# A gated mix of a long convolution and linear attention: the inverse transform of the last channel groups turned by VectorE

## The chip, the cores and the metric

The kernel runs on one core of one Trainium2 chip. The metric is the device time of one launch in microseconds (us), as the median of several runs. The core has five engines that run side by side and meet at semaphores: TensorE (PE: matmuls, and PEld: its weight loads), VectorE (DVE), ScalarE (ACT), GpSimd (POOL) and SyncE (SP), which here only issues DMA transfers. SBUF is the on-chip memory of 128 partitions, PSUM the memory that TensorE writes its results to, DRAM the memory off the core.

## The reference

For a sequence `x` of 2048 steps and 512 channels:

```
g   = sigmoid(sum(x * gate_w))                                   # one number for each step
K   = real(sum_n C * exp(dt*A*l) * dt*B)                         # one kernel of 2048 taps for each channel
a   = irfft(rfft(x, 4096) * rfft(K, 4096))[:2048] + x * Dskip    # causal convolution along the steps
b   = linear attention: softmax features of q and k (32 heads of 16), num / den, then @ wo
out = g * a + (1 - g) * b
```

Data are bf16, sums on the chip f32.

## The kernel before

The convolution is done as a Fourier transform of 4096 points in two stages, in matmuls with small tables. The 512 channels are cut into sixteen **units** of 32 channels (`U` = 0 to 15), four units to a **quarter** (`Q` = 0 to 3). Of each unit the kernel `K` is built first (`kgen`): VectorE multiplies out a table `A` (steps A1, A2, and A3, a sum over two halves of `A`, L1109) and a table `R` (Rh, Rl), both from exponentials `E` (ScalarE, then El on VectorE) and sines `cs` (ScalarE), and TensorE contracts them into `kps`. The string `FOURS` names the units whose A3 is left out, with twice as many matmuls in its place. `kps` is evicted to `KD`, transformed by TensorE (`psA`, evicted to `XA`; `psB`, evicted to `XK`), and VectorE multiplies `XK` with the spectrum of `x`, read back from DRAM as `XUX` (steps t128, t64, t32; L1231, L1234).

Then comes the inverse transform, `transform`. Its first half is one matmul step, `psz`, evicted to `Zr`. Its second half (`psy`, many matmuls with the table `TJ`, 64 rows by 32 columns each) needs two indices of `Zr` exchanged inside blocks of 32 partitions. There are two ways to it:

- the **far** path: `Zr` is written to a DRAM tensor `Zd` (step zw) and read back in the other order as `ZT` (step zr). Quarters 0 to 2 take it in groups of 128 channels; the last quarter for units 12 and 13 together (64 channels) and for unit 14 (32 channels).
- the **narrow** path, for unit 15: 128 matmuls of 64 columns (`pszn`, L1301) give the result in the needed order at once, two evictions give `Z` (Zn), and 128 matmuls of 16 columns follow (`psyn32`, L1358), with two gate products (L1373).

At the end of either, VectorE multiplies by the gate (`ou`, L1367, L1370, L1373) into `xT`, from which the result is stored (L1384).

Attention runs beside it: projections and exponentials of the keys (`pk`, `Ek`), the sums of the exponentials (`Zk`), values (`vp`, evicted to `vb`, then `vr`), and four blocks of queries, the last of which (`late`) is finished near the end (`opsL`, `bpsL`, evictions bs3 and bsg, stores L992). The string `ZPS` names the steps of the keys in which TensorE adds four columns to one first, so that VectorE's reduction (L735) has 512 elements; the others have two reductions of 1024 elements (L732). At the start the channels of `x` are turned (`xT`), copied (`UDp`, step udc), transformed (`psA`, evicted to `XAu`; `psB`, evicted to `xst`, step XU) and written to DRAM (`XUd`).

All steps are nodes of a `Plan`. The order in which they are issued is written out by hand in the string `ORDER`, two characters for a node; each engine works off its nodes in that order. Most evictions may go to ScalarE or VectorE, and `SIDES` has a digit for each: 0 is the first engine named, 1 the second. `RINGS` chooses between PSUM rings in the same way. Rings of buffers (`take` and `drop`) bound how far a step can run ahead; `ax` has one buffer, `Zr` two.

The stores of results name the queues `("SP", "ACT")`; in the code the choice `SP` goes to GpSimd's queue for all stores but the last.

Of the kernel before, what the change touches and what calls it, by code (L numbers as in the profile page):

```python
# [11 lines left out]
ALU = mybir.AluOpType  # L12
# [58 lines left out]
class Plan:  # L71

    DIGITS = "0123456789abcdefghijklmnopqrstuvwxyzABCDEFGHIJKLMNOPQRSTUVWXYZ-_"
    ORDER = ("0405060B0C0D0H0d0e0f0y0z0A190s0t0u0708090I0J0M000L11120g0h0i0j0k0l0K0102030_2R0S0T100W0U0Y2x0V130P0Q2S0N2T0X2y2U142V0O0R"
             "160Z0m0n0o0a0b0c0p0q0r152X2J2Z170-0v0w0x182-1a1b1y1c0E0F0G1n1d2W2K1o2_1e1w1z2Y1H1A2D1x301f2E2L1p1I1E1J1S312M2B2C1g1C3235"
             "361B37381P2F2G2H1q1r1s2I33341F2N2O2v2P2Q2z4C393b3c4J4L3a3d3f4Y4K4M1t1u1v1R3g4-4Z3e4_4N3h4Q3j504R3i4O3l513k4P4S4U3n4V4W1Y"
             "1N3o3m5357584T4X1D5b1G5254593R5c553S5d5e5i5m5j5n3p3r3s5f5g561O5a5q5r5s5h5t5o5x5y1L5k1T4D2w4E3q5u5v5B5l4F5p3w5C3y3x3z3t3u"
             "3v5F5H3D5w5D3F5z1Z5A5E3E5G5U5W5I1U5J5V3A3B3C3G3T5X5M5Q5K3K5R5L4G5S5N3M5_1V1M5Y5O5Z5-63645P5T1Q67606169653N2A683L62663U1W"
             "6a6m6n6o6p1h1i1j3V3W6b1K6c3X6q3Y3Z6r1k1l1m6d3_3-416e6s401X1-3H3I3J4243451_272021442829223O3P3Q47482a4649232d2e4b2b2f244a"
             "2c2o4c252g4g4i2h4h2i4j6f2p2j4d4e4f4k4l4m2q2k2l264n4p4o2m4q2s6t2r4u4v6g2n4r4s4t6i2t4w6h6u4x2u6j8m6k6x8q6v8k8o6y6l6z4y4z4A"  # L80
             "6w6A6B8l8p8n8r8s4B8w8x6G8t8y6I8u4H8C4I6J8v8D8z8A8Z8E6K6L8I6M6H6F6C6D6E8B6N8F8-8J7d6O8_7e6P9b9c9d8Q8R6Q7M8G7f7N6R7g7h6S9k"
             "9l9m6T8H8K7i7O7j8S8L8W937P8T7k8M8N8Xan7Q6U6V6W8Uao7l8V8O7m9e9f9g948P6X6Y6Z7R7n7o8Y907p7S6_7071aeaf91ag92a47q6-7r7s7tap95"
             "7Taha8a972a5ai96akaaat73a675ab77979878ajal999aaua7ac7u7v7w7x74am7976aqaras9n7U9o9vadav9p9waK7C7VaEaw9q7WaL7aaB7b9xaQaM7X"
             "7Y9raRaC7y7z7A7D9y9z9h9i9j7Z9D9Eb5b6b7c5c6aFbX9F7c7Eb_7B9L9Mc0axayaDaH7G9NbYc19A9B9C7IaG9GaI9HazaAaJ7F7H7J7-7_80b-818283"
             "84898bc38c8aaNbZaO9s9t9uaPaSc2aTc7858687c4888d9O8f8gc88ececfaYaZa-7K7Lcbc9cc9Pck8haU8ia_b0b18jcBaVca9I9J9KaWaXcdcgclchcC"
             "b8bgb99Q9R9Sba9T9U9VcsctcicHcjbhbobpdYcDbicId-dZeUcmd_bbbjcncybce0bweV9Ze1cvcwbxb2b3b4cVcWcXe2bkbdbebf9W9X9Ycxco9-cue3e4"
             "czblbmbnbqcpcqdOe5creLcAcEeMbycFa0e6e7e8a1dSa2dTa3brcGcJbsbzcK9_eWeNeOcLcPcQcRe9eaebbAeceRcMcNdPedeeefegcOc_dUbtbubvd0eh"
             "bBbCbDcScTcUePeSeid1eQd7d8dQdfe-dVeTbEbFbGd2d9daeXdge_cYcZc-bHbIbJd3d4d5d6dbdndRdcdddeeYbKdhdWdoezeAeBdieZeCeDeEdXbLdpdj"
             "dkdldmbMf0f1dqdrfAfBfDfEf2f4bNg1f5fCf3fGbOfFg2f6f7fefHdBf8bPfffgdsdtdufIfJg7g3eIeJeKbQf9dvdwdxfafKdydzdAfhfidCg4dEdFfLfb"
             "fcfdfMg8fjfkfldGeFeGeHdHfmfnfog5fNg6fOejekfPfpfqfreldDg9gadLdMdNfQgbgcepdIdJdKemgdgeeneogffRfSfTfUbUbVbWeqbRbSbTggfsfVfW"  # L90
             "fXgighgjftgkglgmgngoeresfYfZf-fxfyfzewexeyfufvfwgqf_gpgreteuevg0gvgwgxgsgtgu")
    SIDES = ("101110000101100010001000101110100001101100001011100000000000000000100010010100101001000010000000000000000000000000000000"
             "00000000000000000000000110110000000000000000011000001")
    RINGS = ("000111101111001111000000000000000000000000100000000000000010001110100000101010101101010110011001010100110010011001111001"
             "11110")
# [714 lines left out]
def plan_queries(P, nc, g, psum, r):  # L810
# [14 lines left out]
    def block(b, late, yn=()):  # L825
# [163 lines left out]
        if late:  # L989
            def st(h):  # L990
                for c in (2 * h, 2 * h + 1):
                    nc.gpsimd.dma_start(out=g.out2d[:, 0:384].rearrange("(q j c) d -> c q j d", q=32, j=16, c=4)[c][:, 4 * b:4 * b + 4],  # L992
                                      in_=xT[32 * c:32 * c + 32, 4 * b:4 * b + 4, 0:3, :].rearrange("p j a d -> p j (a d)"))
            for h in range(2):
                P.dma("outL", 1.2, 2.0, lambda h=h: st(h), on, move=0.8, cnt=2, eng=("SP", "ACT"))
# [61 lines left out]
def plan_conv(P, nc, g, psum, r):  # L1057
# [132 lines left out]
    def transform(XA, ready, Q, off, nd, far, Ls, last, co=0, free=True, split=False):  # L1190

        F = Bag()
        ng, ns, nj, nt = nd // 2, 1024 // nd, min(16, 1024 // nd) if far else 8, min(32, 2048 // nd)
        do = slice(off, off + nd)
        nh, w = max(1, nd // 64), min(nd, 64)
# [4 lines left out]
        if far:  # L1200
            byrow = nd > 64
            F.Zd = g.dram.tile([32, 4, 32, nd] if byrow else [4, 32, 32, nd], BF16, name=f"Zd{Q}_{off}")
        tn, zn, rn, wn = [], [], [], []
        for r0 in range(0, 32, ns):
# [24 lines left out]
            def tt(k=None, r0=r0, box=box, end=end):  # L1229
# [11 lines left out]
                if k != 0:  # L1241
                    box.XK = None
                    if end:
                        F.t = None
                    if not far:
                        F.tt = box.t.rearrange("p k (r d) -> p k r d", d=nd)
                        box.t = None
# [8 lines left out]
            if not far:  # L1256
                continue

            def fi(box=box):
                box.ps = psum([128, 2, 512], "psz")  # L1260
                for hb in range(2):
                    for k in range(2):
                        nc.tensor.matmul(box.ps[:, hb, :], lhsT=fc.TIp[:, k].rearrange("p h a t -> p (h a t)"), rhs=box.t[:, k, 512 * hb:512 * hb + 512],  # L1263
                                         start=(k == 0), stop=(k == 1))
                box.t = None

            def fe(box=box):
                box.Z = g.fpool.tile([128, ns, nd], BF16, name="Zr", tag="Zr", bufs=g.P.k["Zr"])
                o, i = box.Z[:].rearrange("p r d -> p (r d)"), box.ps[:].rearrange("p h z -> p (h z)")
                if nd == 128:  # L1270
                    o, i = box.Z[:].rearrange("p r (h c) -> p h r c", h=2), box.ps[:].rearrange("p h (r c) -> p h r c", c=64)
                box.ps = None
                return o, i

            def fw(r0=r0, box=box):
                if byrow:
                    nc.sync.dma_start(out=F.Zd[r0:r0 + ns].rearrange("r x t d -> (x t) r d"), in_=box.Z[:])
                else:
                    nc.sync.dma_start(out=F.Zd[:, :, r0:r0 + ns, :].rearrange("x t r d -> (x t) r d"), in_=box.Z[:])
                box.Z = None  # L1280
            z = P.add("PE", "psz", fi, [tn[-1]] + ([z] if r0 else []), take=[psq, "Zr"], drop=(["r8"] if (r0 + ns) % nt == 0 else []), rw=("TI", ""))
            zn.append(evict("Zr", fe, [z] + zn[-1:]))
            wn.append(P.dma("zw", 0.45, 2.0, fw, [zn[-1]], drop=["Zr"], move=0.9))
# [10 lines left out]
        def iz(k2, box=box):  # L1294
# [9 lines left out]
            if k2:  # L1304
                F.tt = None
# [325 lines left out]
```

## Time and profile before

| | us |
|---|---|
| median of 3 runs | 260.62 |
| lowest, highest | 259.82, 261.87 |
| the profiled execution | 260.65 |
| its span, first to last instruction | 258.9 |
| VectorE busy | 228.8 (88%) |
| ScalarE busy | 224.5 (87%) |
| TensorE busy | 195.5 (76%) |
| GpSimd busy | 20.0 (8%) |

The span is what the trace covers; the time of the execution is 1.75 us longer. "Busy" of an engine counts instructions that work, not waits or the issuing of transfers (POOL's transfers are counted here as its instructions). In the slices of the profile each digit is the busy share of a fortieth of the span, in tenths. In the timeline a row gives start, duration, engine, line, operation, what is written and read, and in brackets how long the engine sat idle before it and what ended the wait; "issue" means that it waited for nothing that the profile shows. In the groups, the columns behind the shapes are the count, the busy time in all, the mean in ns of one, and the idle time before them.

### The profile page before, as it was taken

The page shows a single profiled execution, that of the slowest core. Times are in us where ns is not written, and L with a number is a line of the kernel's source. Part 1 is how long each engine was busy: PE and PEld are TensorE (multiplying, and loading weights), DVE is VectorE, ACT ScalarE, POOL GpSimd, SP SyncE. Part 2 cuts the span into 40 slices and gives each one's busy share as a digit, 9 for nine tenths or more (in the row PEclk, how much of TensorE's full clock was granted, in tenths as well). Part 3 has the DMA queues.
Part 4 walks back from the last instruction along what each step waited for, and adds up shares of the span by engine and source line. Part 5 has one row for each costly group of instructions (what it writes and reads, how often), then busy time and mean ns, then how long its engine had stood idle before and what let it go on. Part 6 is the DMA issues. An engine that isn't in the chain of part 4 may idle for free. (4 is left out here: it accounts for less than half of the span.)

```text
span 258.9 us, 10101 instructions
## 1 busy us (share of the span) xinstructions
PE 195.5 (76%) x4512; PEld 133.2 (51%) x4512; DVE 228.8 (88%) x308; ACT 224.5 (87%) x312; POOL 20.0 (8%) x37
## 2 busy tenths in 40 slices
PE   0558899999963787689648748688988589979832
PEld 0558664665643533246437434464775456856621
DVE  6798889797899998999999999999989999978711
ACT  7989979998999999999999999999997999766210
POOL 5540000000000000000000000000000000000770
PEclk9999999999998589999997997999999999999975
DMA  6799300073710578304632348615578988896792
GB/s 195 132 189 203 77 4 1 5 228 81 227 39 0 165 206 246 122 4 120 171 98 69 90 135 231 179 36 166 129 153 231 239 186 225 214 251 130 172 197 44
DMA packets 62139, 36.19 MB, mean 140 GB/s; under 512 B 42768, under 2 KB 57296, under 8 KB 61712
## 3 DMA queue, kind: packets, MB, share of 16 engines
q1 hardware_dynamic: 60272, 33.58, 52.4%
q0 software_dynamic: 768, 1.84, 3.1%
q8 instruction: 35, 0.57, 1.0%
q10 hardware_dynamic: 1056, 0.13, 0.3%
q14 instruction: 8, 0.07, 0.1%
HBM read 22.17 MB, written 13.37 MB: 137 GB/s over the span
## 5 line engine op out<-in xcount | busy, mean ns | idle before, releaser
L1098 DVE TENSOR_TENSOR A<-Ctab,Dtab 128x2048 bf16<-128x2048 bf16 x32 | 38.6, 1220 | 1.2 <-PE kps L179 1.2
L68 ACT ACTIVATE cs<-args 128x1024 bf16<-128x1024 f32 x32 | 31.3, 1073 | 0.0
L1384 POOL DMA_DIRECT2D out_dram<-xT x12 | 7.7, 649 | 225.0 <-ACT xT L145 223.4
L179 PE MATMUL kps<-R,A 128*32 128x64 bf16 x1536 | 17.6, 202 | 6.2 <-DVE A L1109 1.4
L179 PEld LDWEIGHTS <-A 128*32 128x32 bf16 x1536 | 15.8, 117 | 10.2 <-DVE R L1120 2.9
L1120 DVE TENSOR_TENSOR R<-E,cs 128x2048 bf16<-128x2048 bf16 x16 | 19.4, 1218 | 0.0
L1116 DVE TENSOR_TENSOR R<-E,cs 128x2048 bf16<-128x2048 bf16 x16 | 19.3, 1220 | 0.1
L1263 PE MATMUL psz<-t,TI 128*128 128x512 bf16 x60 | 16.2, 396 | 3.0 <-ACT cs L68 1.6
L145 ACT CAST XK<-psB 128x1024 bf16<-128x1024 f32 (+1 forms) x17 | 16.8, 1016 | 0.9 <-PE psB L192 0.8
L145 ACT CAST Zr<-psz 128x1024 bf16<-128x1024 f32 x15 | 15.6, 1040 | 2.1 <-ACT cs L68 0.6
L1231 DVE TENSOR_TENSOR t<-XUX,XK 128x2048 bf16<-128x2048 bf16 x14 | 17.1, 1219 | 0.0
L68 ACT ACTIVATE E<-args 128x1024 bf16<-128x1024 f32 x16 | 17.0, 1065 | 0.0
L68 ACT ACTIVATE Eq<-pq 128x512 bf16<-128x512 f32 (+1 forms) x28 | 16.8, 696 | 0.2 <-PE pq L839 0.2
L68 ACT ACTIVATE Ek<-pk 128x512 bf16<-128x512 f32 x32 | 16.7, 602 | 0.2
L753 PE MATMUL vp<-WW,xT 128*128 128x512 bf16 x64 | 16.8, 395 | 0.0
L612 PE MATMUL psB<-XAu,TB 64*128 64x128 bf16 x256 | 11.3, 250 | 6.2 <-ACT XAu L145 4.1
L839 PE MATMUL pq<-xT,Wqp 128*128 128x512 bf16 x64 | 15.4, 380 | 0.3 <-ACT E L68 0.3
L145 ACT CAST XA<-psA 128x1024 bf16<-128x1024 f32 x15 | 15.2, 1053 | 0.4 <-PE psA L186 0.4
L705 PE MATMUL pk<-WW,xT 128*128 128x512 bf16 x64 | 15.2, 380 | 0.0
L612 PEld LDWEIGHTS <-TB 64*128 64x128 bf16 x256 | 9.7, 111 | 9.5 <-issue 9.0
L762 DVE TENSOR_TENSOR vr<-vb,vr 128x1024 bf16<-128x1024 bf16 x16 | 10.6, 688 | 3.0 <-ACT vr L68 2.7
L186 PE MATMUL psA<-W,KD 128*64 128x128 bf16 x256 | 10.0, 223 | 4.3 <-ACT XK L145 1.7
(208 smaller groups left out, 511.2 us busy)
## 6 DMA issues: line engine op xcount, KB each, us to landing
XUX<-XUd SPq DMA_DIRECT2D x32, 256.0 KB, 4.4
XUd<-xst SPq DMA_DIRECT2D x8, 512.0 KB, 3.3
ax<-apd SPq DMA_DIRECT2D x16, 256.0 KB, 4.9
Zd<-Zr SPq DMA_DIRECT2D x15, 256.0 KB, 4.5
ZT<-Zd SPq DMA_DIRECT2D x12, 256.0 KB, 4.7
UD<-in_A_u_dram SPq DMA_DIRECT2D x16, 128.0 KB, 4.7
XUd<-xst SPq DMA_DIRECT2D x8, 256.0 KB, 3.9
wqk<-in_B_wqkv_dram SPq DMA_DIRECT2D x1, 1024.0 KB, 6.7
```

What stands on the lines that cost most here:

```text
L68: return self.nc.scalar.activation(**kw)
L145: self.nc.scalar.copy(out=o, in_=i)
L179: nc.tensor.matmul(kps[32 * dj:32 * dj + 32, g4, e, :], lhsT=A[:, d // 4, 32 * ka:32 * ka + 32, d % 4], rhs=R[:, kr, d, :], start=(i == 0) ...
L612: nc.tensor.matmul(box.ps[:, c2, sl, :], lhsT=fc.TB[rows, b0:b0 + 2].rearrange("p a b -> p (a b)"), rhs=X.t[rows, k, r0 + sl].rearrange("p ...
L705: nc.tensor.matmul(box.ps[:], lhsT=xT[:, st, kt, :], rhs=g.WW[:, kt, :], start=(kt == 0), stop=(kt == 3))
L753: nc.tensor.matmul(box.ps[:], lhsT=xT[:, st, kt, :], rhs=g.WW[:, 4 + kt, :], start=(kt == 0), stop=(kt == 3))
L839: nc.tensor.matmul(box.ps[:, m - m0, :] if late else box.ps[:], lhsT=g.Wqp[:, kt, 128 * m:128 * m + 128], rhs=xT[:, 4 * b:4 * b + 4, kt, : ...
L1098: nc.vector.tensor_tensor(out=c.A[:, :, 64 * k:64 * k + 64, :].rearrange("p q (x b) l -> p x b q l", b=8), in0=cf.unsqueeze(2).to_broadcas ...
L1116: nc.vector.tensor_tensor(out=c.R[:, :, :, 32:64], in0=t.E[:, 1].unsqueeze(1).to_broadcast([128, 2, 32, 32]), in1=t.cs[:], op=ALU.mult)
L1120: nc.vector.tensor_tensor(out=c.R[:, :, :, 0:32], in0=t.E[:, 0].unsqueeze(1).to_broadcast([128, 2, 32, 32]), in1=t.cs[:, ::-1, :, ::-1], o ...
L1231: nc.vector.tensor_tensor(out=box.t, in0=Ls[r0 // ns].X[:], in1=box.XK[:].unsqueeze(1).to_broadcast([128, 2, 1024]), op=ALU.mult)
L1263: nc.tensor.matmul(box.ps[:, hb, :], lhsT=fc.TIp[:, k].rearrange("p h a t -> p (h a t)"), rhs=box.t[:, k, 512 * hb:512 * hb + 512], start= ...
```

## The change

Units 12 and 13, unit 14 and unit 15 all take one path: `psz` as in the far path, evicted to `Zr`, and then `nc.vector.transpose` on VectorE turns each block of 32 partitions by 32 elements, from SBUF to SBUF (a new step, Zt). `Zd` and `ZT` remain for quarters 0 to 2 only. For units 12 and 13 the source and the result of the turn lie in the halves of one `ax` buffer, for 14 and 15 in `Zr` buffers. The narrow path is gone; unit 15 goes through `psz` in two halves (pszh) with two evictions (Zh), and through the `psy` matmuls that unit 14 has.

Besides, `ORDER`, `SIDES`, `RINGS`, `FOURS` and `ZPS` are new throughout, and the stores of results choose between SP and POOL, each digit now naming the queue that is used.

```diff
-    FOURS = ("0111100101011000")
-    ZPS = ("01000111")
+    FOURS = ("1000111001101100")
+    ZPS = ("00000001")
...
-                    nc.gpsimd.dma_start(out=g.out2d[:, 0:384].rearrange("(q j c) d -> c q j d", q=32, j=16, c=4)[c][:, 4 * b:4 * b + 4],
+                    (nc.gpsimd if P.cur.at == "POOL" else nc.sync).dma_start(out=g.out2d[:, 0:384].rearrange("(q j c) d -> c q j d", q=32, j=16, c=4)[c][:, 4 * b:4 * b + 4],
...
+        turn = nd < 128
+        ring = "Zr" if nd == 32 else "ax"
+        if not turn:
+            F.Zd = g.dram.tile([32, 4, 32, nd], BF16, name=f"Zd{Q}_{off}")
...
+            def fe(k=None, r0=r0, box=box):
+                if turn and nd == 64:
+                    if r0 == 0:
+                        F.ax = g.fpool.tile([128, 4096], BF16, name="ZT", tag="ax", bufs=g.P.k["ax"])
+                        F.Zr = F.ax[:, 0:2048].rearrange("p (r d) -> p r d", d=64)
...
+            if split:
+                z = P.add("PE", "pszh", lambda fi=fi: fi((0,)), tn[:1] + ([g.turned] if ring == "Zr" else []), take=[psq] + tk, rw=("TI", ""))
+                zh = P.add("PE", "pszh", lambda fi=fi: fi((1,)), [z] + tn, drop=dr, rw=("TI", ""))
+                zn += evict2("Zh", fe, [[], [zh]], z)
                 continue
...
+        def fs():
+            if nd == 32:
+                F.Z = g.fpool.tile([128, 32, 32], BF16, name="Zt", tag="Zr", bufs=g.P.k["Zr"])
+            else:
+                F.Z = F.ax[:, 2048:4096].rearrange("p (t d) -> p t d", d=64)
+                F.ax = None
+            nc.vector.transpose(out=F.Z[:].rearrange("p t d -> p d t"), in_=F.Zr[:].rearrange("p r d -> p d r"))
+            F.Zr = None
...
+        if turn:
+            rn = [P.add("DVE", "Zt", fs, zn + ([g.turned_y] if nd == 32 and split else []), take=(["Zr"] if nd == 32 else []), drop=(["Zr"] if nd == 32 else []))] * 2
+            g.turned = rn[0]
...
-        def iz(k2, box=box):
-            if k2 == 0:
-                F.Z = g.wk.tile([128, 64, ng], BF16, name="Z", tag="A", bufs=g.P.k["A"])
-                box.ps = psum([128, 2, 64, 8], "psz")
-            for gg in range(8 * k2, 8 * k2 + 8):
-                for k in range(2):
-                    for x in range(4):
-                        nc.tensor.matmul(box.ps[32 * x:32 * x + 32, gg // 8, :, gg % 8], lhsT=F.tt[:, k, :, ng * (x // 2) + gg],
...
-                    (nc.scalar if P.cur.at == "ACT" else nc.sync if last else nc.gpsimd).dma_start(out=ov[c][:, js], in_=...)
+                    (nc.gpsimd if P.cur.at == "POOL" else nc.sync).dma_start(out=ov[c][:, js], in_=...)
...
-                    P.dma("out", 1.2, 2.0, lambda h=h, st=st: st(h), on, move=(1.6 if pair else 1.05 if far and nd == 128 else 0.9), cnt=2, eng=("SP", "ACT"))
+                    P.dma("out", 1.2, 2.0, lambda h=h, st=st: st(h), on, move=(1.6 if pair else 1.05 if nd == 128 else 0.9), cnt=2, eng=("SP", "POOL"))
...
-        g.LAST = (((12, 13), True), ((14,), True), ((15,), False))
+        g.LAST = ((12, 13), (14,), (15,))
```

More of the change, by code (lines that the diff above doesn't have):

```diff
@@ L1255, in transform, with fi @@
                 tn.append(P.add("DVE", "t%d" % nd, tt, x + [Ls[r0 // ns].n] + tn[-1:], drop=["XK", Ls[r0 // ns].ring]))
[L1256 to L1261, printed above, removed]
+            def fi(hs=(0, 1), box=box):
+                if 0 in hs:
+                    box.pz = psum([128, 2, 512], "psz")
+                for hb in hs:
                     for k in range(2):
[L1263 removed]
+                        nc.tensor.matmul(box.pz[:, hb, :], lhsT=fc.TIp[:, k].rearrange("p h a t -> p (h a t)"), rhs=box.t[:, k, 512 * hb:512 * hb + 512],
@@ L1409, in plan_conv @@
         if h % 2:
-            transform(XA, done, h // 2, 0, 128, True, [load(h // 2, p) for p in range(4)], False)
+            transform(XA, done, h // 2, 0, 128, [load(h // 2, p) for p in range(4)], False)
     for n in yn:
@@ L1417, in plan_conv @@
     L, first = [load(3, p) for p in range(4)], None
-    for k, (units, far) in enumerate(g.LAST):
+    for k, units in enumerate(g.LAST):
         XA = Bag()
```

170 lines of the change are left out of this document (70 added, 100 removed).

## The prediction

> **What bounds the kernel now.** I read the page's busy shares first, then the slices, then stretches cut by hand at 236.1 us, where VectorE ends the last sum over table `A` (for channel unit 15), and at 254.46 us, where it ends its last instruction.
>
> ```profile
> PE 195.5 (76%) x4512; PEld 133.2 (51%) x4512; DVE 228.8 (88%) x308; ACT 224.5 (87%) x312; POOL 20.0 (8%) x37
> DVE  6798889797899998999999999999989999978711
> ACT  7989979998999999999999999999997999766210
> 0.00:20.00 20.00, 7.67 (x68) 7.06 (x69) 15.63 (x40) 16.86 (x22) 10.13 (x21) 1.00 0.85 173
> 20.00:60.00 40.00, 38.02 (x629) 25.77 (x628) 35.55 (x52) 37.13 (x64) 0.00 (x0) 1.00 0.38 90
> 60.00:100.00 40.00, 29.80 (x521) 19.50 (x520) 36.01 (x62) 38.90 (x57) 0.00 (x0) 0.87 0.43 123
> 100.00:236.10 136.10, 107.52 (x2775) 72.29 (x2775) 131.87 (x143) 127.14 (x163) 0.00 (x0) 0.97 0.60 155
> 236.10:254.46 18.36, 12.53 (x525) 8.54 (x523) 9.69 (x15) 4.51 (x10) 9.88 (x16) 0.85 0.79 153
> 254.46:258.90 4.44, 0.00 (x0) 0.00 (x0) 0.01 (x1) 0.00 (x0) 0.00 (x0) 0.50 0.37 59
> sum 258.90, PE 195.54 PEld 133.16 DVE 228.76 ACT 224.54 POOL 20.01; mean PE 32.59 PEld 22.19 DVE 38.13 ACT 37.42 POOL 3.34
> ```
>
> In a stretch's row the engines follow its length as PE, PEld, DVE, ACT, POOL. From 100 to 236.1 us VectorE works 131.87 of 136.10 us: it is the bound there, with ScalarE close behind. Ahead of 100 us it idles 4.37 + 4.45 + 3.99 = 12.8 us, so ahead of 236.1 us it idles 17.0 and works 219.06. Behind that point it works 9.69 of 18.36 us: a chain through several engines is the bound. The last 4.44 us are the output transfer. The timeline shows the chain:
>
> ```profile
> 215.50 1.22 DVE L1231 TENSOR_TENSOR t<-XUX,XK 128x2048 bf16<-128x2048 bf16 x1
> 224.68 1.74 SPq L1289 DMA_DIRECT2D ZT<-Zd  x4
> 232.34 0.63 PE L1345 MATMUL psy<-ZT,TJ 64*32 64x128 bf16 x32 [0.52 <-DMA ZT<-Zd]
> 234.87 1.23 DVE L1109 TENSOR_TENSOR A<-A 128x2048 bf16<-128x2048 bf16 x1
> 236.84 0.73 PE L179 MATMUL kps<-R,A 128*32 128x64 bf16 x64
> 237.50 1.04 PE L1263 MATMUL psz<-t,TI 128*128 128x512 bf16 x4
> 238.47 0.64 PE L186 MATMUL psA<-W,KD 128*64 128x128 bf16 x16
> 241.21 0.95 PE L192 MATMUL psB<-XA,TB 128*128 128x32 bf16 x32
> 242.20 1.07 ACT L145 CAST XK<-psB 128x512 bf16<-128x512 f32 x2 [0.42 <-PE psB L192]
> 242.82 1.29 DVE L1234 TENSOR_TENSOR t<-XUX,XK 128x1024 bf16<-128x1024 bf16 x2 [1.33 <-ACT XK L145]
> 243.29 5.67 SPq L1289 DMA_DIRECT2D ZT<-Zd  x4
> 244.17 1.98 PE L1301 MATMUL psz<-TI,t 128*32 128x64 bf16 x123 [0.95 <-DVE t L1234]
> 248.04 0.33 PE L1301 MATMUL psz<-TI,t 128*32 128x64 bf16 x5 [1.89 <-issue]
> 252.31 0.22 PE L1358 MATMUL psy<-Z,TJ 64*32 64x16 bf16 x9 [1.28 <-issue]
> 253.01 0.69 PE L1345 MATMUL psy<-ZT,TJ 64*32 64x32 bf16 x64
> 253.77 0.69 DVE L1370 TENSOR_TENSOR xT<-psy,gT 128x512 bf16<-128x512 f32 x1 [0.74 <-PE psy L1345]
> 254.54 1.62 ACTq L1384 DMA_DIRECT2D out_dram<-xT  x2
> 254.55 1.33 SPq L1384 DMA_DIRECT2D out_dram<-xT  x2
> ```
>
> After its last product (243.46 to 244.11) unit 15 takes 128 small matmuls, two evictions and 128 more small matmuls, with two gaps in which TensorE waits for nothing that the profile names: 1.89 and 1.28 us. Only then come unit 14's last matmuls and VectorE's last instruction.
>
> **The change part by part.** All of `ORDER`, `SIDES`, `RINGS`, `FOURS` and `ZPS` is new, so I read the strings out against the list of steps and counted, engine by engine. The prices:
>
> ```profile
> L732 DVE TENSOR_REDUCE Zk<-Ek 128x64 f32<-128x1024 bf16 x8 | 9.4, 1212 | 0.0
> L735 DVE TENSOR_REDUCE Zk<-zk 128x128 f32<-128x512 f32 x4 | 2.7, 686 | 0.6 <-PE zk L726 0.6
> L147 DVE CAST XAu<-psA 128x1024 bf16<-128x1024 f32 x9 | 10.6, 1218 | 2.7 <-PE psA L587 2.7
> L145 ACT CAST XAu<-psA 128x1024 bf16<-128x1024 f32 x7 | 7.1, 1009 | 0.4 <-PE psA L587 0.3
> L147 DVE CAST vb<-vp 128x512 bf16<-128x512 f32 x4 | 2.7, 686 | 0.1
> L145 ACT CAST vb<-vp 128x512 bf16<-128x512 f32 x12 | 7.2, 598 | 0.3 <-DVE vr L762 0.2
> L980 DVE TENSOR_SCALAR xT<-bps,gT 128x384 bf16<-128x384 f32 x4 | 2.3, 610 | 0.0
> L1373 DVE TENSOR_TENSOR xT<-psy,gT 128x256 bf16<-128x256 f32 x2 | 0.8, 424 | 5.9 <-PE psy L1358 5.9
> L147 DVE COPY UDp<-UD 128x1024 bf16<-128x1024 bf16 x7 | 2.8, 419 | 0.0
> L265 DVE TENSOR_SCALAR tgv<-tgc,one 128x1024 int32<-128x1024 f32 x2 | 3.2, 1593 | 0.0
> DMA to landing us min/median/max: 3.0/4.9/6.8
> ```
>
> *Transpositions.* Three are added on VectorE: 128x2048 for units 12 and 13, 128x1024 each for 14 and 15. No row shows one. The dearest row of 128x1024 elements is 1.593 us, the cheapest a 0.419 us copy. I take the reduction's 1.21 us, an instruction that also turns its input's order and reads element by element; for the double size twice that less about 0.15 of fixed cost (0.686 for 128x512 against 1.212 for twice as much), so 2.27. Together 4.7 us; the bounds are 1.5 and 6.3.
>
> *VectorE's total.* `ZPS` falls from four ones to one: three steps exchange one short reduction for two long, 3 x (2 x 1.212 - 0.686) = +5.2 (TensorE loses 24 matmuls). `SIDES` moves four XAu evictions to ScalarE (-4.9), five vb to VectorE (+3.4), three oT to ScalarE (3 x 0.686 as vb: -2.1); the small ones (two bsg, a bs3 and half an XA away, one Y, xT and UDp copy to it) sum to -0.8. Two table builds swap VectorE for GpSimd and back, taken as nothing. Unit 15's two gate products of 0.424 become one of 0.69: -0.2. `FOURS` keeps eight ones, so sums over `A` and kernel matmuls keep their number. Sum: 4.7 + 5.2 - 4.9 + 3.4 - 2.1 - 0.8 - 0.2 = +5.3 us, total 234.1.
>
> *What stands behind unit 15's sum over A.* In the new order these VectorE steps do: one 1.22 us product of unit 12/13, two gate products of the third quarter and its Y eviction (1.22, 0.69, 0.69), unit 14's two products and half an XA (3 x 0.65), the turn of 2.27, two products of unit 15 (1.3), the turn of unit 14 (1.21), two bsg (1.2), a gate product of 1.22, unit 15's turn (1.21) and two gate products of 0.69. That is 15.6 us; before it was 9.69. So 234.1 - 15.6 = 218.5 us stand ahead of the point, before 219.06. With the same idle time the point comes at 235.5, not 236.1.
>
> *The tail behind it*, walked through with the rows above, from the point as zero. TensorE makes the kernel matmuls (0.73), the two inverse steps of 12/13 (until 2.9, the second waits for VectorE's product), psA 3.5, then the late attention block's matmuls, which took 2.3 us at 239.03, to 5.9, psB 6.9. VectorE reaches the first turn at 5.8 without a wait (its input's second `Zr` eviction ends near 5), ends it at 8.0, makes one product, then waits some 0.4 us for unit 14's `Zr` (psz 7.9, eviction of 1.04), and has its remaining work stacked from there; unit 15's own inverse is four matmuls and two 0.59 us evictions beside it, hidden. So VectorE, idle for half of this stretch before, becomes its bound: last gate product ends at 15.6 + 0.4 = 16.0, not 18.36. The two gaps of TensorE go with the 256 small matmuls.
>
> *Transfers.* The writes and reads of `Zd` for the last groups go (three writes, eight reads). Most result stores move from GpSimd's queue to SP's, some twelve at 0.645 (half of 1.33) each, in the place of the `ZT` issues. The last stores stand all four on SP: 2.6 us of issues, not 1.62 in parallel; +1.0. Nothing is queued behind them. SP's earlier stores end before the last product, about 15 against 16.
>
> *Sum.* 235.5 + 16.0 + 4.44 + 1.0 = 256.9 us of span. The profiled execution took 260.65 us with a span of 258.9, so 1.75 lie around it; it stands 0.03 above the median of 260.62. That gives 258.7. The idle time ahead of the point is the unknown: ahead of 100 us VectorE gets 5.2 - 4.9 + 3.4 + 1.1 = +4.8 us and ScalarE, the nearer bound there, loses about 1.6 (+4.0 XAu, -3.0 vb, -2.1 copies, a -0.6 step moved later). None of the 4.8 need go into the 12.8 us of gaps, or all of it may. I let 0.5 fill gaps: **258.2 us**.
>
> [...] The two gaps are 128 pairs of weight load and matmul apart: 5 narrow ones behind the first, then 2, 64, 2 and 55 (249.53 to 251.04), so 256 instructions. [...]
>
> **The rivals.**
> *The gaps fill.* All 4.8 us of early work fall into VectorE's idle time: 258.7 - 4.8 = 253.9. For it: 12.8 us idle there, and TensorE, busy 38.02 of 40 us from 20 to 60, is relieved. Against: ScalarE idles only 7.1 us in the first 100 and loses just 1.6.
> *The third quarter's read comes late (slower).* It still goes through DRAM. Before, its last inverse matmuls began at 232.34, 15.6 us after the product that feeds them (ended 216.72), and 19.4 us lay between that product and the point. In the new order only 16.7 us of VectorE work lie there (twelve of 1.22, three of 0.69), and the kernel matmuls of unit 15 and the gate products are queued behind those inverse matmuls on TensorE. Cover falls to about 0.5 us behind their 0.63. Four such issues took 1.74 us here and 5.67 elsewhere, landing 4.9 at the median and 6.8 at most: 3.9 + 1.9 - 0.5 = 5.3 us more, 264.0. It decides once the read is over 0.5 us later.
> *TensorE's gaps stay* though the small matmuls go: unit 14's and 15's 64-matmul bursts stand at the end. 1.89 + 1.28 on the chain: 258.7 + 3.2 = 261.9.
> *The change doesn't do what it says*, or the turn runs at another pace: at 0.419 a kilo-element some 1.6 us less (much of the first turn is covered by unit 14's wait), at 1.593 1.6 more, 256.6 to 259.8.
>
> **How the numbers follow.** The forecast gets 0.48, of itself 256.4 to 260.4; filled gaps 0.25; the late read 0.13; TensorE's gaps 0.08; another pace 0.06. Only what moves over 1%, below 258.0 or above 263.2, can be told from no change. Faster: 0.4 of the forecast's half, nearly all of the filled gaps: 0.43. Slower: half of the late read and a little of the rest: 0.10. Same: 0.47. The range reaches from the filled gaps to the far side of the staying gaps, 253.9 to 262.0; below lies under half of the first rival, above most of the second.
>
> **What would show it.** Right: three transpositions of about 2.3, 1.2 and 1.2 us; no `Zd` traffic after the third quarter; VectorE at nine tenths until 5 to 6 us before the end; fourteen long reductions on L732's line and five XAu casts; the last stores four in a row on SP. Wrong: a DMA wait ahead of the third quarter's last inverse matmuls, idle VectorE ahead of 100 us far from 12.8, or PE gaps by "issue" behind the last turn. The forecast falls if a turn costs over 2 us per 128x1024, or if the rewritten order leaves ScalarE rather than VectorE last.

## The result and the profile after: 5.6% slower

| | before | after |
|---|---|---|
| median, us | 260.78 (259.82 to 261.87, 4 runs) | 275.15 (273.82 to 277.19, 4 runs) |
| ratio | | 1.0557, 95% interval [1.0466, 1.0647] |
| profiled execution, span | 260.65, 258.9 | 277.19, 275.4 |

The forecast was 258.2 us with a range to 262.0. Medians here are of all executions, while ratios and intervals leave out slow ones, over 1.5% above the fastest of their version, so the two do not always agree. The profiled execution of after is the slowest of its four, 2.0 us above the median; a difference of a us or two in its stretches can be its own. First the busy shares and the slices of after, VectorE's above all (to be read beside those of before):

```profile
PE 200.7 (73%) x4298; PEld 131.7 (48%) x4298; DVE 248.2 (90%) x311; ACT 227.7 (83%) x315; POOL 11.5 (4%) x24
...
DVE  6799899999999959999999999689999998869991
ACT  7789999999999999998999899869998976553010
```

VectorE works 19.4 us more than before, at nine tenths nearly to the end, while ScalarE falls from five tenths to none over the last six slices (one is 6.9 us). Cut at the two places that the prediction used, the end of the last sum over `A` and the end of the last gate product:

```profile
0.00:100.00 100.00, 73.46 (x1110) 48.13 (x1111) 90.09 (x155) 93.54 (x138) 8.85 (x20) 0.93 0.51 121
100.00:237.55 137.55, 109.88 (x2818) 74.56 (x2817) 129.72 (x141) 125.63 (x165) 0.00 (x0) 0.91 0.56 146
237.55:269.96 32.41, 17.33 (x372) 9.05 (x371) 28.36 (x17) 8.55 (x15) 2.63 (x4) 0.70 0.33 65
269.96:275.40 5.44, 0.00 (x0) 0.00 (x0) 0.01 (x1) 0.00 (x0) 0.00 (x0) 0.50 0.29 48
```

The stretch ahead of the point is 2.5 us longer than forecast (237.55 against 235.5 less 0.5), the last one exactly as forecast (5.44 us), and the middle one has twice its forecast length: 32.41 against 16.0 us, VectorE busy in 28.36 of it. The groups say with what:

```profile
L1305 DVE STREAM_TRANSPOSE ZT<-ZT 128x2048 bf16<-128x2048 bf16 x1 | 9.5, 9470 | 0.0
...
L1305 DVE STREAM_TRANSPOSE Zt<-Zr 128x1024 bf16<-128x1024 bf16 x2 | 9.3, 4632 | 0.6 <-ACT Zr L145 0.6
...
L732 DVE TENSOR_REDUCE Zk<-Ek 128x64 f32<-128x1024 bf16 x14 | 16.4, 1210 | 0.0
...
L147 DVE CAST XAu<-psA 128x1024 bf16<-128x1024 f32 x5 | 5.9, 1219 | 0.6 <-PE psA L587 0.6
```

The three turns take 18.7 us, not 4.7: 4.5 to 4.6 ns for each element in a partition, where the dearest row of the page before had 1.6. The other counts are those of the forecast: fourteen long reductions, five XAu casts. The timeline shows the turns in the way of everything behind them:

```profile
239.00 0.51 PE L1344 MATMUL psy<-ZT,TJ 64*32 64x128 bf16 x22 [1.63 <-issue]
...
240.09 3.39 PE L1259 MATMUL psz<-t,TI 128*128 128x512 bf16 x8
...
246.06 9.47 DVE L1305 STREAM_TRANSPOSE ZT<-ZT 128x2048 bf16<-128x2048 bf16 x1
...
255.97 4.61 DVE L1305 STREAM_TRANSPOSE Zt<-Zr 128x1024 bf16<-128x1024 bf16 x1
...
256.11 1.03 PE L1259 MATMUL psz<-t,TI 128*128 128x512 bf16 x2 [5.82 <-DVE t L1234]
```

During the first turn VectorE owes unit 15's product `t`, and TensorE stands 5.82 us for it. The first row, 1.63 us without a named reason, is a second matter, to which the experiments come back.

### The profile page after: what moved, and what is told of

It is laid out like the page before. It is cut to its first block, busy times and chain, and to the rows that moved or that the text cites. A ratio compares the mean times of both kernels' runs of the same rounds, so it can differ in the third digit from the quotient of the medians.

```text
span 275.4 us, 9674 instructions
## 1 busy us (share of the span) xinstructions
PE 200.7 (73%) x4298; PEld 131.7 (48%) x4298; DVE 248.2 (90%) x311; ACT 227.7 (83%) x315; POOL 11.5 (4%) x24
## 5 line engine op out<-in xcount | busy, mean ns | idle before, releaser
L1259 PE MATMUL psz<-t,TI 128*128 128x512 bf16 x64 | 20.1, 447 | 12.7 <-DVE t L1234 8.6
L145 ACT CAST Zr<-psz 128x1024 bf16<-128x1024 f32 (+1 forms) x15 | 14.6, 980 | 13.4 <-PE psz L1259 12.8
L179 PE MATMUL kps<-R,A 128*32 128x64 bf16 x1536 | 17.0, 202 | 6.4 <-ACT xT L145 2.8
L179 PEld LDWEIGHTS <-A 128*32 128x32 bf16 x1536 | 15.4, 116 | 10.5 <-issue 6.2
L1120 DVE TENSOR_TENSOR R<-E,cs 128x2048 bf16<-128x2048 bf16 x16 | 19.4, 1217 | 0.0
L753 PE MATMUL vp<-WW,xT 128*128 128x512 bf16 x64 | 18.5, 420 | 0.0
L145 ACT CAST XA<-psA 128x1024 bf16<-128x1024 f32 (+1 forms) x16 | 16.0, 1015 | 2.5 <-PE psA L186 2.4
L839 PE MATMUL pq<-xT,Wqp 128*128 128x512 bf16 x64 | 17.7, 423 | 0.0
L732 DVE TENSOR_REDUCE Zk<-Ek 128x64 f32<-128x1024 bf16 x14 | 16.4, 1210 | 0.0
L705 PE MATMUL pk<-WW,xT 128*128 128x512 bf16 x64 | 16.0, 380 | 0.0
L1259 PEld LDWEIGHTS <-TI 128*128 128x128 bf16 x64 | 6.4, 107 | 19.9 <-issue 10.2
L929 PE MATMUL ops<-Eq,KVbd 128*128 128x256 bf16 x64 | 10.5, 308 | 3.6 <-ACT Eq L68 3.0
```

The source lines that it names most:

```text
L145: self.nc.scalar.copy(out=o, in_=i)
L179: nc.tensor.matmul(kps[32 * dj:32 * dj + 32, g4, e, :], lhsT=A[:, d // 4, 32 * ka:32 * ka + 32, d % 4], rhs=R[:, kr, d, :], start=(i == 0) ...
L732: nc.vector.tensor_reduce(out=K.Z[:, u].rearrange("p g h -> p (g h)"), in_=K.E[:, u].rearrange("p g (h f) -> p (g h) f", f=16), axis=mybir ...
L753: nc.tensor.matmul(box.ps[:], lhsT=xT[:, st, kt, :], rhs=g.WW[:, 4 + kt, :], start=(kt == 0), stop=(kt == 3))
L839: nc.tensor.matmul(box.ps[:, m - m0, :] if late else box.ps[:], lhsT=g.Wqp[:, kt, 128 * m:128 * m + 128], rhs=xT[:, 4 * b:4 * b + 4, kt, : ...
L1120: nc.vector.tensor_tensor(out=c.R[:, :, :, 0:32], in0=t.E[:, 0].unsqueeze(1).to_broadcast([128, 2, 32, 32]), in1=t.cs[:, ::-1, :, ::-1], o ...
```

## Experiments: what a turn costs

Three theories of this price for an element. *Far steps*: the turn as written steps through its source and its result with 64 or 128 bytes between neighbours. *One pace*: a transposition costs this for each element, however it lies. *Fixed price*: it costs so much for each 32x32 block.

**bench_turns** takes the operations out of the kernel. Each is one VectorE instruction on data in SBUF, `d` being 32 or 64 channels:

```diff
+dense:   transpose(out=t.rearrange("p (d t) -> p d t", t=32), in_=src.rearrange("p (d r) -> p d r", r=32))
+fromfar: transpose(out=t.rearrange("p (d t) -> p d t", t=32), in_=src.rearrange("p (r d) -> p d r", d=d))
+tofar:   transpose(out=t.rearrange("p (t d) -> p d t", d=d),  in_=src.rearrange("p (d r) -> p d r", r=32))
+pairs:   transpose of the same bytes as 32-bit elements, each two neighbouring channels, side by side
+cfrom, cto: tensor_copy with the far steps on one side
```

> Nothing of the reference is computed: sixteen VectorE instructions alone, one after another, turns of 32x32 blocks with runs of 32 elements laid side by side or far apart (64 or 128 bytes from element to element), on either side, and copies with the same steps. Theory A, the far steps cost: turns with both sides side by side take 1.2 us for 128x1024 and 2.3 for 128x2048, those far on one side lie between, both far 4.6 and 9.5 as in the changed kernel; the copy with the same far steps is slow too. Theory B, the instruction has one pace whatever the layout: all turns of 128x1024 take 4.6 us, also side by side. Theory C, a fixed price for each block of 32x32 (4.6 us / 32 = 0.145): like B, but turns of pairs (two bf16 moved as one 32-bit element, half as many blocks) take 2.3 us; by B the pairs take 4.6 x 512/1024 = 2.3 as well if the price is by element, by A 0.7.

Its timeline (start, duration; the first row and that of pairs hold a small and a double instruction):

```profile
4.22 3.44 DVE L26 STREAM_TRANSPOSE dense<-src 128x1024 bf16<-128x1024 bf16 x2 [4.22 <-DMA src<-in_A_u_dram]
7.58 1.84 DVE L31 STREAM_TRANSPOSE fromfar<-src 128x1024 bf16<-128x1024 bf16 x1
9.35 4.58 DVE L36 STREAM_TRANSPOSE tofar<-src 128x1024 bf16<-128x1024 bf16 x1
...
27.21 1.99 DVE L46 STREAM_TRANSPOSE pairs<-src 128x512 f32<-128x512 f32 x2
...
31.87 1.00 DVE L56 COPY cfrom<-src 128x1024 bf16<-128x1024 bf16 x1
32.76 2.41 DVE L56 COPY cto<-src 128x1024 bf16<-128x1024 bf16 x1
...
40.58 9.25 DVE L36 STREAM_TRANSPOSE tofar<-src 128x2048 bf16<-128x2048 bf16 x1
```

Side by side, 3072 elements take 3.44 us, the pace that the prediction took. Read far apart, 1024 take 1.84; written far apart, 4.58, and 9.25 for the double size: the kernel's own 4.63 and 9.47. So it is the far steps, and above all on the side that writes; far reads add 0.6 us. The other two theories fall: pace and number of blocks are the same in all three rows of 1024.

**turn_dense** lets the eviction ahead of the turn write each channel's 32 values side by side, so that the turn has no far steps:

```diff
-    F.Zr = F.ax[:, 0:2048].rearrange("p (r d) -> p r d", d=64)
+    F.Zr = F.ax[:, 0:2048].rearrange("p (d r) -> p r d", r=32)
...     # units 14 and 15 and the turns' results in the same way
```

> The change with one edit: the evictions lay Zr out channel by channel and the turn writes the same way, so each turn reads and writes runs side by side; the matmuls behind it read with a step of 64 bytes instead. Theory A: turns of 1.2, 1.2 and 2.3 us, 14 us less on VectorE, of which some 13 on the path: 261 to 262 us. Theory B or C: turns as before, 275 us.

Measured: 274.93 us (274.61 to 275.66), ratio to before 1.0596 [1.055, 1.0642]. The groups:

```profile
L1310 DVE STREAM_TRANSPOSE Zt<-Zr 128x1024 bf16<-128x1024 bf16 x2 | 2.5, 1245 | 7.2 <-ACT Zr L145 7.2
...
L1310 DVE STREAM_TRANSPOSE ZT<-ZT 128x2048 bf16<-128x2048 bf16 x1 | 2.3, 2311 | 3.3 <-ACT ZT L145 3.3
...
L145 ACT CAST ZT<-psz 128x1024 bf16<-128x1024 f32 x2 | 9.3, 4632 | 1.1 <-PE psz L1259 1.1
```

The turns now have the forecast's prices, 1.245 and 2.311 us, and nothing is won: the evictions that write the far steps take 4632 ns on ScalarE, to the nanosecond what the turn took on VectorE, and VectorE waits 10.5 us for them. The price goes with the write: another engine and another operation pay it too. That it is the same for every operation is not so: VectorE's copy with far results (`cto` above) took 2.41 us, half of it.

**turn_pairs** turns two neighbouring channels as one 32-bit element. The eviction then writes them as pairs, and the matmuls behind read pairs:

```diff
-    nc.vector.transpose(out=F.Z[:].rearrange("p t d -> p d t"), in_=F.Zr[:].rearrange("p r d -> p d r"))
+    nc.vector.transpose(out=z.bitcast(F32).rearrange("p (e t) -> p e t", t=32), in_=F.zr.bitcast(F32).rearrange("p (e r) -> p e r", r=32))
...     # the evictions' results and the operands of the matmuls behind, in pairs
```

> As turn_dense, but two neighbouring channels are moved as one 32-bit element: half the elements and half the blocks. Theory A: turns of 0.7, 0.7 and 1.2 us, about 260 us. Theory B by element or C by block: half of the turns' time goes, 9.3 us, 266 us.

Measured: 263.06 us (261.84 to 263.69), ratio 1.0119 [1.0063, 1.0175]. The groups:

```profile
L1312 DVE STREAM_TRANSPOSE Zt<-Zr 128x512 f32<-128x512 f32 x2 | 1.4, 712 | 1.1 <-ACT Zr L145 1.1
...
L1312 DVE STREAM_TRANSPOSE ZT<-ZT 128x1024 f32<-128x1024 f32 x1 | 1.2, 1239 | 0.0
...
L145 ACT CAST ZT<-psz 128x1024 bf16<-128x1024 f32 x2 | 2.1, 1042 | 1.1 <-PE psz L1259 1.1
```

The turns take 2.7 us, and the evictions are back at 1042 ns although their pairs lie 128 bytes apart. The turns have the prices of theory A, but the time is 3 us above its 260. Of the 5.6% that the change cost, 1.2% are left.

**copy_for_turn** has a plain copy in the place of the turn (the 32x32 blocks are left unturned), the cheapest that this step could be:

```diff
-    nc.vector.transpose(out=F.Z[:].rearrange("p t d -> p d t"), in_=F.Zr[:].rearrange("p r d -> p d r"))
+    nc.vector.tensor_copy(out=F.Z[:], in_=F.Zr[:])
```

> The changed kernel with a plain copy in the place of each turn, so the blocks are not turned. Copies of 0.42, 0.42 and 0.7 us by the rows of before, 17 us less on VectorE. If the turns are all that the prediction had wrong, this comes where the prediction put a turn at a copy's pace: 256.6 us. If the rewritten order costs by itself, it stays above: 258 to 260 us, as the point behind unit 15's sum came 2.0 us later than forecast and the tail had 2.3 us beside the turns.

Measured: 262.04 us (259.55 to 264.99), ratio 1.0062 [1.0019, 1.0105]. The groups:

```profile
L1305 DVE COPY Zt<-Zr 128x1024 bf16<-128x1024 bf16 x2 | 0.9, 426 | 1.0 <-ACT Zr L145 1.0
...
L1305 DVE COPY ZT<-ZT 128x2048 bf16<-128x2048 bf16 x1 | 0.7, 686 | 0.0
```

The copies have the price that was expected, and the time is above both expectations. The prediction had 256.6 for a turn at this pace. So a second error of some 5 us stands beside the turn's price, and it lies in the rest of the change.

**bench_strides** asks how far "far" is: the turn of 128x1024 with its results written 2 to 64 bytes apart, the same in 32 bits, and ScalarE's copy.

```diff
+transpose(out=t.rearrange("p (D t s) -> p D s t", s=s, t=32), in_=src.rearrange("p (D s r) -> p D s r", s=s, r=32))   # s = 1, 2, 4, 8, 16, 32
```

> Nothing of the reference is computed; the operations stand by themselves. VectorE's turn of 128x1024 bf16, read side by side, whose neighbouring results are written 2, 4, 8, 16, 32 or 64 bytes apart; the same as 128x512 of 32 bits, written 4, 8, 16 or 64 bytes apart; and ScalarE's copy of 128x1024 bf16 with the results 2 to 64 bytes apart. Theory 'lines of 16 bytes': up to 8 bytes apart (two results or more in a line) a turn stays at 1.2 to 1.3 us, from 16 bytes on it costs 4 to 4.6, of bf16 and of 32 bits alike (0.71 us side by side, 2.2 or more far apart). Rival 'a result of less than 32 bits that has no neighbour beside it': already at 4 bytes apart the bf16 turn costs 4 us or more, whatever the distance, and the 32-bit turn stays within 0.7 to 1.1 us at every distance. ScalarE as VectorE in both cases (1.0 side by side, 4.6 at 64 bytes).

VectorE's timeline (start, duration):

```profile
5.38 1.27 DVE L27 STREAM_TRANSPOSE wtwo<-src 128x1024 bf16<-128x1024 bf16 x1
6.54 2.40 DVE L27 STREAM_TRANSPOSE wfour<-src 128x1024 bf16<-128x1024 bf16 x1
8.75 4.73 DVE L27 STREAM_TRANSPOSE weight<-src 128x1024 bf16<-128x1024 bf16 x1
...
17.40 4.98 DVE L27 STREAM_TRANSPOSE wthirtytwo<-src 128x1024 bf16<-128x1024 bf16 x1
...
24.26 1.04 DVE L27 STREAM_TRANSPOSE fsixteen<-src 128x512 f32<-128x512 f32 x1
```

ScalarE's timeline of the same run, at 16 bytes:

```profile
8.54 4.80 ACT L32 COPY aeight<-src 128x1024 bf16<-128x1024 bf16 x1
```

The number in a tile's name is the distance in elements (`w` and `a` of 16 bits, `f` of 32). Both theories miss: a 16-bit result costs nothing more at 4 bytes (1.27), double at 8 bytes (2.40), four times at 16 (4.73), and no more beyond (4.98 at 64); ScalarE's copies run nearly the same way (1.04 side by side, then 1.33, 2.46, 4.80, and 5.07 at 64 bytes). 32-bit results take 1.08 us for 512 elements at 16 bytes and 1.04 at 64, against 0.92 at 4 and 0.70 at 8. In these rows a 16-bit result costs 4.6 to 5.0 ns when it is written 16 to 64 bytes from the next, 2.3 to 2.4 at 8 bytes, and 1.2 to 1.3 at 4, for VectorE's transposition and ScalarE's copy alike. It is not a rule for every write: turn_pairs' evictions wrote two results side by side, the pairs 128 bytes apart, and took 1.042 us for 128x1024, and VectorE's copy with far results took 2.41.

## Experiments: the other 5 us

What turn_pairs shows against the forecast, cut in the same way:

```profile
100.00:237.51 137.51, 108.34 (x2820) 73.67 (x2819) 130.24 (x142) 126.62 (x165) 0.00 (x0) 0.93 0.57 148
237.51:256.41 18.90, 15.62 (x372) 9.13 (x371) 12.93 (x18) 8.73 (x15) 2.62 (x4) 0.91 0.48 95
256.41:261.80 5.39, 0.00 (x0) 0.00 (x0) 0.00 (x0) 0.00 (x0) 0.00 (x0) 0.53 0.46 67
```

Behind the point 18.90 us, where the forecast had 16.0 and would have had 14 at these turns' prices. VectorE works 12.93 of them, TensorE 15.62: TensorE is the bound. Its timeline there:

```profile
237.06 0.34 PE L1355 MATMUL psy<-ZT,TJ 64*32 64x128 bf16 x10
239.23 0.51 PE L1355 MATMUL psy<-ZT,TJ 64*32 64x128 bf16 x22 [1.83 <-issue]
239.67 1.05 PE L179 MATMUL kps<-R,A 128*32 128x64 bf16 x64
240.65 3.09 PE L1259 MATMUL psz<-t,TI 128*128 128x512 bf16 x8
243.67 0.64 PE L186 MATMUL psA<-W,KD 128*64 128x128 bf16 x16
```

And the two microseconds behind the gap as a stretch (the granted clock is the last column but two):

```profile
240.00:242.00 2.00, 2.00 (x60) 1.08 (x49) 2.00 (x3) 0.65 (x2) 0.00 (x0) 0.50 0.03 9
```

In the midst of the third quarter's last 32 matmuls TensorE stops for 1.83 us, then runs at a granted clock of 0.50, and the eight inverse matmuls of units 12 and 13 take 3.09 us (four took 1.04 before). `psA` of unit 15 ends 6.8 us behind the point; the forecast had 3.5.

Two theories of the rest: *order*, that TensorE's work was moved behind the point by the new `ORDER` and meets its gap there; or *the way itself*, that going through the turn is no shorter than the narrow matmuls.

**pairs_shifted** adds 64 small matmuls far ahead of the tail:

```diff
+    if g.extra:     # in the first eight psA steps
+        g.extra -= 1
+        for i in range(8):
+            nc.tensor.matmul(box.ps[:, i, 0:32], lhsT=g.ident[:], rhs=g.ident[:, 0:32], start=True, stop=True)
...
+        g.extra = 8
```

> As turn_pairs, with 64 small matmuls more (128 instructions of TensorE, in the first eight steps that transform a kernel, whose results are overwritten). Theory 'blocks of 256 instructions': the gap of 1.83 us that stood after the 10th of 32 matmuls of the third quarter's last multiplication goes from there and appears, if at all, 64 matmuls earlier or later in TensorE's sequence (near the 42nd matmul of the last kernel's generation, or between 231 and 235 us); time 261.5 to 264. Rival 'the gap belongs to that place' (what it waits for isn't in the trace): it stays after the 10th of the 32.

TensorE's timeline around the last kernel's matmuls:

```profile
239.23 0.55 PE L179 MATMUL kps<-R,A 128*32 128x64 bf16 x42
242.76 0.45 PE L179 MATMUL kps<-R,A 128*32 128x64 bf16 x22 [2.97 <-issue]
```

The queue of instructions among the DMA queues of its page (packets, MB, share of 16 engines' span):

```profile
q8 instruction: 34, 0.56, 0.9%
```

The gap left its place, and one stands behind the 42nd of the 64 kernel matmuls, exactly 64 matmuls on: 22 were left of the 32. Counted from the first matmul, turn_pairs has its gaps behind number 3542 and 3926, this run behind 2007, 3030, 3926 and 4054, the kernel before behind 4309 and 4437, each 85 to 87 past a multiple of 128. So a gap belongs to a count of instructions (256, since each matmul has its weight load), not to a step, and the one shown is the next boundary of that count. The queue fits: 34 packets for 2 x 4362 instructions on TensorE, 257 to a packet. The DMA records of before and after fit that such a packet is what is waited for: their four gaps over 0.8 us end 1.3 us after a packet of that queue has landed (before: landed at 246.73 and 251.05, gaps to 248.04 and 252.31; after: 222.36 and 237.73, gaps to 223.70 and 239.00).

Most of the 34 packets go by without a gap of over 0.6 us; the four such gaps of this run took 0.74 to 2.97 us.

The time, expected at 261.5 to 264, was 270.51 (267.06 to 271.72; before 258.95 beside it). In the profiled execution (267.06) there are four gaps, of 0.80 near 148 us, 2.41 near 199, 0.74 and 2.97, where turn_pairs had 1.49 and 1.83. Where these boundaries fall may be worth some us by itself. How much of the difference to turn_pairs the gaps account for, and how much the 64 matmuls, was not separated.

**pairs_no_stores** asks if the block comes late because the DMA engines are full; the eight stores that SP issues from 233 us are left out.

```diff
     def st(h, js=slice(0, 12 if Q < 3 else 16)):
+        if nd == 128:
+            return
```

> As turn_pairs, without the eight stores of the second and third quarters' results that SP issues from 233 to 247 us (those results don't reach DRAM). Theory 'the block of instructions comes late because the DMA engines are full' (their busy share was 0.96 to 1.07 from 234 to 238 us, 0.40 when the gap ended): the gap of 1.83 us shrinks to under 0.5 and the time falls by 1.5 to 2.5 us, to 260.5 to 261.5. Rival 'the fetch takes its time whatever the DMA engines do': gap within 1.3 to 2.4 us, time 262 to 264.

TensorE's timeline at the third quarter's last matmuls:

```profile
239.86 0.51 PE L1355 MATMUL psy<-ZT,TJ 64*32 64x128 bf16 x22 [1.88 <-issue]
```

And the DMA engines ahead of it (their share is the last column but one):

```profile
236.00:238.00 2.00, 1.98 (x59) 1.77 (x57) 2.00 (x2) 0.94 (x2) 0.00 (x0) 1.00 1.03 361
```

Measured: 263.4 us (262.6 to 264.55). The gap stayed, in place and length: these stores aren't its cause. But the engines were as full without them (1.03, against 1.07 in turn_pairs) while the block's packet was under way (237.30 to 238.40), so the theory of full engines is not settled by this run. What makes some blocks late stays open.

**pairs_old_sums** puts the feature sums of three units back on TensorE:

```diff
-    ZPS = ("00000001")
+    ZPS = ("01000111")
```

> As turn_pairs (263.1 us), but the feature sums of three more units stand on TensorE again, as in the kernel before, the order of work unchanged. If VectorE's total sets the time up to the point, its 5.2 us of reductions go and the time falls by 3 to 5 us, to 258 to 260. If ScalarE or TensorE binds as often there, the point moves by under 1.5 us and the time stays within 261.5 to 264.

Measured: 265.29 us (261.48 to 266.05), ratio 1.0185 [1.0073, 1.0298]. VectorE's 5.2 us brought nothing that shows, but its 24 matmuls also move every later boundary, and four gaps of 0.97 to 2.78 us came up, the longest in another kernel's matmuls near 222 us. It can't tell the worth of the sums: inconclusive.

**old_order** goes the other way: the turn in pairs within the order, sides, rings, sums and store queues of before. Only what the turn needs is moved (the inverse matmuls of 12 and 13 behind the third quarter's, whose `ax` buffer they take over).

```diff
-    FOURS = ("1000111001101100")
-    ZPS = ("00000001")
+    FOURS = ("0111100101011000")
+    ZPS = ("01000111")
...     # ORDER, SIDES, RINGS and the queues of the stores as before
```

> The transposition with two neighbouring channels as one 32-bit element, put into the order of work of the kernel before: its sequence, its choice of engines, of PSUM rings and of sums on TensorE, its stores on GpSimd's and ScalarE's queues. Only what the transposition itself requires is moved: the matmuls and evictions of groups 12 and 13 stand behind the last multiplication of the third quarter, whose buffer they take over. Theory 'TensorE behind the point' (the rewritten order left TensorE without a pause from 240 to 250 us, so the tail is 18.9 us long whatever VectorE does): here the matmuls and products ahead of the point come as before (point at 236 to 238 us), the last gate product ends at 249.5 to 251 us, the span is 254 to 256 and the time 255.5 to 258 us, some 6 us below the same transposition in the new order (263.1). Rival 'the way through the transposition is itself no shorter than the way through TensorE's narrow matmuls': 260 us or more, with the last gate product at 254 or later.

Measured: 259.94 us, ratio 1.0031 [0.9995, 1.0067]: 0.9% below turn_pairs and level with before, not the expected 255.5 to 258. Its profiled execution took 263.5 us, 3.6 above the median, so I read from it the order of events, not the durations:

```profile
250.56 0.71 DVE L1312 STREAM_TRANSPOSE Zt<-Zr 128x512 f32<-128x512 f32 x1 [1.25 <-ACT Zr L145]
251.20 1.10 DVE L980 TENSOR_SCALAR xT<-bps,gT 128x384 bf16<-128x384 f32 x2
...
252.22 1.28 DVE L1366 TENSOR_TENSOR xT<-psy,gT 128x512 bf16<-128x512 f32 x2
...
254.96 1.13 POOL L992 DMA_DIRECT2D out_dram<-xT  x2
```

I had put two products of the linear branch (L980) behind the last turn, though their sums were ready before it; GpSimd's last stores wait for them and are issued until 256.09, behind the last gate product at 253.50.

**old_order_mended** moves these two ahead of the turn:

```diff
  ORDER of VectorE:
-    ... Zt_15, bsg, bsg, ou_15, ou_14
+    ... bsg, bsg, Zt_15, ou_14, ou_15
```

> As old_order (259.9 us against 258.95 of the kernel before), with two places of VectorE's order mended: the two products of the linear branch that stood behind the last turn go ahead of it (their sums were ready 4 us earlier, and GpSimd's four last stores waited for them until 256.1 us), and the gate product of unit 14 comes ahead of that of unit 15. Theory 'order, not the turn': VectorE fills the 1.25 us in which it waited for the eviction, the last gate product ends 0.7 to 1 us earlier, GpSimd's stores are issued by 253.5 instead of 256.1, the end follows the last product by 4.4 us instead of 7.3, and the time falls by 2.5 to 3.5 us, to 256 to 257.5: faster than the kernel before by 0.5 to 1.2%. Rival 'the end is set by the bytes that are left to store, wherever they are issued': within 0.7 us of old_order.

Measured: 259.47 us (257.07 to 261.19), ratio 0.9984 [0.9947, 1.0021]. The expected 256 to 257.5 was missed; within 0.7 us of old_order is what the rival had. From its profiled execution (257.83, 1.6 below the median):

```profile
248.71 0.69 DVE L1366 TENSOR_TENSOR xT<-psy,gT 128x512 bf16<-128x512 f32 x1 [0.29 <-PE psy L1355]
...
250.12 1.13 POOL L992 DMA_DIRECT2D out_dram<-xT  x2
```

The last gate product ends at 249.40, 5.1 us ahead of before, but the span only at 256.1; GpSimd's queue still issues stores until 251.25.

**old_order_stores** gives the four stores of groups 12 and 13 to SP, idle by then:

```diff
-    (nc.scalar if P.cur.at == "ACT" else nc.sync if last else nc.gpsimd).dma_start(
+    (nc.scalar if P.cur.at == "ACT" else nc.sync if last or nd == 64 else nc.gpsimd).dma_start(
```

> As old_order_mended (259.5 us; in its profiled execution the last gate product ended at 249.40 us, 5.1 earlier than in the kernel before, but GpSimd issued stores until 251.25 and the span ended at 256.1, 6.7 us behind the product instead of 4.4). The four stores of groups 12 and 13 go from GpSimd's queue to SP's, which is idle there. Theory 'the end is now GpSimd's queue of stores': its last issue comes by 249.5, the end follows the last product by 4.4 to 5 us, the time falls by 1.5 to 2.5 us, to 257 to 258, 0.6 to 1.1% below the kernel before. Rival 'the bytes are late, not their issue' (the DMA engines' busy share was 0.80 and 1.13 from 250 to 254 us): within 0.7 us of old_order_mended.

The stretches from the point to the last gate product and to the end:

```profile
235.78:251.07 15.29, 13.24 (x350) 8.23 (x349) 11.97 (x18) 6.70 (x12) 7.25 (x12) 1.00 0.46 95
251.07:256.80 5.73, 0.00 (x0) 0.00 (x0) 0.00 (x0) 0.00 (x0) 0.04 (x1) 0.63 0.64 120
```

Measured: 258.68 us (256.76 to 260.62; before 259.83 beside it), ratio 0.9956 [0.9917, 0.9996]. The gain over old_order_mended is 0.8 us, not the expected 1.5 to 2.5, and the two intervals overlap. It is the only version whose interval lies below before's time, by 0.4% in the middle and by almost nothing at its upper end. So the turn can stand in for the narrow path at no loss; that the 0.4% are its own is not shown, since the kernel before was not run with its stores moved likewise. The tail is 15.29 us (18.36 before), TensorE runs at a clock of 1.00 there, and the end takes 5.73 instead of 4.44. I put that down to stores that now follow each other closely (DMA share 0.64 in that stretch, 0.37 before), which no run isolates.

## Why the prediction was wrong, by its own steps

- **The turn's price failed**, and with it the time. It was put at 4.7 us with bounds of 1.5 to 6.3 and took 18.7. The nearest row (L732, a reduction that the prediction took to turn the order of its *input*; the code sums sixteen neighbours in the order in which they lie) had the price of a transposition that writes side by side, 1.21 against 1.245, though why the two agree no run shows; but the diff's output pattern steps 64 or 128 bytes between neighbours, and no row that was used showed the price of such writes. The bounds came from rows, but from rows of another access pattern: neither end bounded this one. The text named the number on which it would fall, 2 us for 128x1024; it was 4.63.
- **VectorE's other terms held.** Forecast total 234.1 us; with the turns at their measured price 234.1 + 18.7 - 4.7 = 248.1, measured 248.2.
- **The point came 2.5 us late** (237.55 against 235.0): 1.3 us more work ahead of it (219.8 instead of 218.5) and 1.2 more of idle time. The 1.3 are an error of my count: the steps behind the point are the ones that I listed, but I took the sum of their single durations from a total of busy time, in which rows that overlap count once (after: 30.25 us as single rows, 28.36 busy). Ahead of 100 us VectorE idled 9.9 us instead of 12.8, so 2.9 of the 4.8 did fill gaps, as the first rival had it; but from 100 us to the point it idled 7.8 instead of 4.2 and gave it back.
- **The tail's bound was wrong.** 32.41 - 16.0 = +16.4 us: 14.0 from the turns, less the 1.3 above, and 3.7 of idle time (4.05 against 0.4). I had VectorE as the bound from the first turn on. With the turn cheap (turn_pairs) it is TensorE that works without a pause from 239.2 to 253.7, behind a gap that the forecast had struck out.
- **The two gaps of TensorE** were read rightly as 256 instructions apart and then let go with the small matmuls. They belong to the count, not to those matmuls: in after two came up where the count reaches a boundary, 0.87 us near 223 and 1.63, behind matmul 3542 and 3926. The rival that kept them, at 0.08, was right in kind and had the wrong place; a granted clock of 0.58 in after and 0.50 in turn_pairs behind the gap (240 to 242 us) came on top.
- **The late read** did not come: no wait for a transfer stands ahead of the third quarter's last matmuls; the gap splits them (10 and 22).
- **The last stores**, four in a row on SP: +1.0 forecast, 5.44 us for the end measured, as put down.

The cause of the result is shown: 5.6% slower becomes 1.2% when 32-bit pairs are written. That the remaining 1.2% come with the new order and what was rewritten beside it (sides, rings, sums, store queues) is shown by the three runs in the old order, which lose them with the turn kept. How they split between gaps, clock and moved steps is read from the timelines, not isolated. One rival stands: the gaps alone could be most of it, since those over 0.6 us sum to 3.3 us in turn_pairs and to none, 1.6 and 1.0 us in the profiled executions of the three, and a new order moves every boundary.

## What to carry to other kernels

Before pricing an operation read its output's access pattern: 128x1024 16-bit results written 16 to 64 bytes apart took about four times the dense time here, 4.69 to 4.98 us against 1.25 in a transposition on VectorE, 4.80 to 5.07 against 1.04 in ScalarE's copies and 4.63 against 1.04 in its evictions. Moving the far steps to the instruction ahead only moved the bill (274.93 us against 275.15); transposing pairs as 32-bit elements removed it (0.71 us). Where a stretch has a chain and not a bound, count every engine's work in it: with the turns at 2.7 us instead of 18.7, the tail's bound went from VectorE (28.36 of 32.41 us) to TensorE (15.62 of 18.90). After a change of instruction counts look for new gaps without a releaser at multiples of 256 instructions before blaming the step in which they stand: those placed here lay 85 to 87 matmuls past a multiple of 128, whatever the step.

## What I had not expected of the hardware

- 16-bit results 2, 4, 8, 16 and 64 bytes apart: 1.25, 1.27, 2.40, 4.73 and 4.98 us for 128x1024, in a transposition, with ScalarE's copies at 4.80 for 16 bytes; reading far apart took 1.84 against 1.25 side by side.
- A VectorE copy whose results are far apart takes 2.41 us, half of the transposition's 4.58 with the same writes.
- TensorE's gaps without a releaser stood 85 to 87 matmuls past a multiple of 128 wherever they were counted (before, after, turn_pairs, pairs_shifted), and the four over 0.8 us in before and after end 1.3 us after a packet of instructions has landed. With 64 matmuls more ahead of the tail, the gap before the end stood 64 matmuls on and took 2.97 us instead of 1.83, and every execution was at least 3.3 us slower than the slowest of turn_pairs.
